# Summing all but the last key head's output products at full width in one bank, with output weights in longer runs

## The chip, the cores and the metric

The kernel runs on one core of a Trainium2 chip. The time is the device time in microseconds of one execution of the whole program, given as the median of several runs.

## What is computed

One decode step for two sequences (B = 2) of width D = 448. A layer norm of the input feeds a sliding-window attention over a key and value cache and a dense layer with a mish activation; both are added to the input. The attention has 16 query heads and 8 key heads of 256 numbers, and looks at the last 4096 positions.

```python
x = A_x                                   # (2, 1, 448), all inputs bf16
xn = _layernorm(x, axis=-1)
q = (xn @ wq)                             # 16 query heads of 256
k, v = last 4096 positions of the caches  # 8 key heads, each for two query heads
p = softmax(q @ k.T * 256 ** -0.5)
attention = (p @ v, heads side by side) @ wo       # wo: 4096 x 448
h = xn @ w1 + b1                          # 1792 wide
dense = (h * tanh(softplus(h))) @ w2
return x + attention + dense
```

The caches are by far the most of what is read: 8 key heads, each with 4 MB of K and 4 MB of V for both sequences, beside 3.5 MB of query weights, 3.1 MB of dense weights and 3.5 MB of output weights.

## The kernel before, in words

Key heads are the outer loop. For key head `i`, K and V (4 MB each) and the 448 KB of output weights that belong to its two query heads are loaded on the SP queue (`load_k`, `load_v`, `load_wo`, L349 and L366), one head ahead of their use. K and V have two buffers each, the output weights three; a load is issued when the buffer's last reader is done, and all loads queue behind each other.

A key head's 4096 positions lie as 64 rows in the 64 partitions of each sequence. They are worked on in four pieces of 16 rows (`NH` = 4 pieces, `T` = 64):

- `turn` (L373): VectorE transposes a piece of K in 32x32 blocks, one piece ahead.
- `scores` (L385): eight TensorE products of 128x512 for a piece, summed in one bank, with the query laid out block-diagonally (`qdiag`, built by GpSimd at L266). ScalarE takes the exponential in two halves (L399) and sums as it goes.
- `turn_p` (L411): VectorE transposes the exponentials of the piece before; after a head's last piece it forms the sums for the denominator (L418, L420).

After the four pieces of head `i`, the values of head `i-1` follow. `denominator` (L427) sums over partitions with an fp32 product, and VectorE takes the reciprocal (L431). Then for heads 0 to 5 `values` (L444) runs 32 products with the probabilities stationary (8 columns: two rows of positions times four (sequence, query head) pairs) and V moving, into an 8x512 bank, which ScalarE copies to `o_sb` (L452). For the last two heads (`NFIX` = 2) `values_fixed` (L494) has V stationary instead: 128 products of four columns, whose result is already transposed.

`finish` (L475 to L479) belongs to heads 0 to 5 and runs one head later, after the first piece's scores of head `i+2`: TensorE transposes the 8x512 result with four fp32 transposes, VectorE adds the two row halves, and `scale_o` (L458) multiplies by the reciprocal. `values_fixed` calls `scale_o` directly. `mix` follows: for each of two query heads and two halves of 256, the two columns of `oT` (one per sequence) are the stationary operand and the output weights move.

The sum of everything that goes to the output (the input, the dense layer, eight heads) lives in PSUM all through the kernel. `add` (L217) splits the 448 columns in four groups of 112, each on its own 32 columns of TensorE's array and its own 32 partitions of PSUM, in two banks (`psA0`, `psA1`). So each `add` is four products. At the end VectorE copies two groups to `res` and ScalarE the other two (L563), and SP stores them (L564).

`issue_in_order` ties every engine's instructions to the order in which the program writes them, so on each engine the order in the code is the order on the chip. The main loop at the end of the kernel therefore sets the order around the change: in head `i`'s iteration, loads for `i+1` and `i`, then per piece `turn` of the next, `scores`, `turn_p` of the one before, and after the first piece `close(i-2)`, which is `finish` and `mix`; after the pieces, the values of `i-1`. In the ninth iteration: `close(6)`, the values of head 7, `close(7)`.

Of the kernel before, what the change touches and what calls it, by code (L numbers as in the profile page):

```python
# [9 lines left out]
ALU = mybir.AluOpType  # L10
AXIS = mybir.AxisListType
BF16 = mybir.dt.bfloat16
FP32 = mybir.dt.float32
# [21 lines left out]
def kernel(  # L35
# [30 lines left out]
    BR = Bsz * rep  # L66
# [6 lines left out]
    ND = Dh // P  # L73
# [9 lines left out]
    ident = lead.tile([P, P], BF16)  # L83
# [15 lines left out]
    x_bf = consts.tile([Bsz, D], BF16)  # L99
# [13 lines left out]
    for lo, hi in ((0, SC), (SC, NS)):  # L113
# [4 lines left out]
    ident_f = consts.tile([Q, Q], FP32)  # L118
# [11 lines left out]
        out=rstd[:], in_=mv[:, 1:2], func=ACT.Sqrt, bias=eps_t[:], scale=1.0  # L130
# [21 lines left out]
    for j in range(1, NQ):  # L152
        nc.vector.tensor_tensor(
            out=hsel, in0=hsel, in1=ident[:, j * Q : (j + 1) * Q : HS], op=ALU.add
# [4 lines left out]
    for b in range(Bsz):  # L159
        nc.vector.tensor_reduce(  # L160
            out=off[:, b : b + 1], in_=hsel[:, b * rep : (b + 1) * rep], axis=AXIS.X, op=ALU.add
# [3 lines left out]
    nc.vector.tensor_scalar(  # L165
        out=off[:], in0=off[:], scalar1=mine[:], scalar2=1e4, op0=ALU.subtract, op1=ALU.mult
    )
    ones_f = consts.tile([P, P], FP32)
    nc.gpsimd.memset(ones_f[:], 1.0)
    NW = 2  # L170
# [8 lines left out]
    for s in range(NS):  # L179
# [7 lines left out]
        out=odd[:],  # L187
        in_=ident[:].rearrange("p (u o) -> p o u", o=2),
        axis=AXIS.X,
        op=ALU.add,  # L190
    )
    xs = consts.tile([P, NS, NX, Bsz], BF16)
    for par in range(2):
        for x in range(NX):
            which = (par + x) % 2
            nc.vector.tensor_scalar(
                out=xs[:, par : NS : 2, x, :],
                in0=xnT_ps[:, par : NS : 2, :],
# [5 lines left out]
    nc.vector.memset(ones[:], 1.0)  # L204

    NO = NQ
    DO = D // NO
    psA = [ps_a.tile([P, DO], FP32, name=f"psA{u}") for u in range(2)]  # L210

    def part(n):
        return psA[n // 2][n * Q : n * Q + Bsz, :]

    def add(lhsT, w, start=False, stop=False):
        for n in range(NO):
            nc.tensor.matmul(  # L217
                part(n),
                lhsT=lhsT,
                rhs=w[:, n * DO : (n + 1) * DO],  # L220
                start=start,
                stop=stop,
                tile_position=(0, n * Q),
                skip_group_check=True,
            )

    add(ident[0:Bsz, 0:Bsz], x_bf[:, :], start=True)


    xq = consts.tile([P, NS, NQ, Q], BF16)  # L230
# [107 lines left out]


    NSTEP = Hkv * NH  # L340
    k_t, kt_t, v_t, p_t, pT_t, wo_t = {}, {}, {}, {}, {}, {}
    state = {}

# [7 lines left out]
    def load_k(i, cuts=(0, T)):  # L351
        k_t[i] = k_pool.tile([P, T * Dh], BF16, tag="k", name="k")
        load_cache(k_t[i], A_k_cache, i, cuts)

    def load_v(i, cuts=(0, T)):
        t = v_tile()
        load_cache(t, A_v_cache, i, cuts)
        v_t[i] = t[:].rearrange("p (t d) -> p t d", t=T)

    def load_wo(kvh, parts=1):  # L360
        w = wo_pool.tile([P, rep, ND * D], BF16, tag="wo", name="wo")
        r0 = kvh * rep * Dh
        win = A_wo[r0 : r0 + rep * Dh, :].rearrange("(h p c) d -> p h (c d)", h=rep, p=P)
        for u in range(parts):
            hs = slice(u * rep // parts, (u + 1) * rep // parts)
            nc.sync.dma_start(out=w[:, hs, :], in_=win[:, hs, :])  # L366
        wo_t[kvh] = w

    def turn(s):
        kt = kt_pool.tile([P, TH * Dh], BF16, tag="kt", name="kt")  # L370
        i, half = divmod(s, NH)
        k = k_t[i] if half < NH - 1 else k_t.pop(i)
        nc.vector.transpose(  # L373
            out=kt[:].bitcast(FP32),
            in_=k[:, half * TH * Dh : (half + 1) * TH * Dh].bitcast(FP32),
        )
        kt_t[s] = kt
# [47 lines left out]
    def denominator(i):  # L425
        den = ps_m.tile([P, BR], FP32, tag="m", name="den")
        nc.tensor.matmul(  # L427
            den[:], lhsT=ones_f[:], rhs=state.pop(("sums", i))[:], start=True, stop=True
        )
        rec = small.tile([P, BR], FP32, tag="rec", name="rec")  # L430
        nc.vector.reciprocal(out=rec[:], in_=den[:])  # L431
        return rec

    NP = 2
    NR = NP * BR

    def values(i):

        po = ps_o.tile([NR, NP * Dh], FP32, tag="o", name="o")
        v = v_t.pop(i)  # L440
        state["rec", i] = denominator(i)
        for u in range(T // NP):
            piece, uh = divmod(u, TH // NP)
            nc.tensor.matmul(  # L444
                po[:],
                lhsT=pT_t[i * NH + piece][:, uh * NP * Q : (uh + 1) * NP * Q : HS],
                rhs=v[:, u * NP : (u + 1) * NP, :].rearrange("p t d -> p (t d)"),
                start=(u == 0),
                stop=(u == T // NP - 1),
            )  # L450
        o_sb = small.tile([NR, NP * Dh], FP32, tag="o_sb", name="o_sb", bufs=1)
        nc.scalar.copy(out=o_sb[:], in_=po[:])  # L452
        state["o", i] = o_sb

    def scale_o(i, o):
        rec = state.pop(("rec", i))
        oT = small.tile([P, ND, rep, Bsz], BF16, tag="oT", name="oT")
        nc.vector.tensor_tensor(  # L458
            out=oT[:].rearrange("p c h b -> p c b h"),
            in0=o.rearrange("p c (b h) -> p c b h", b=Bsz),  # L460
            in1=rec[:]
            .rearrange("p (b h) -> p b h", b=Bsz)
            .unsqueeze(1)
            .to_broadcast([P, ND, Bsz, rep]),
            op=ALU.mult,
        )
        state["oT", i] = oT

    def finish(i):
        ov = state.pop(("o", i))[:].rearrange("r (u m c) -> r u c m", u=NP, c=ND)  # L470
        pq = ps_q.tile([P, NP * ND * NR], FP32, tag="q", name="q")
        pqv = pq[:].rearrange("p (u c r) -> p u c r", u=NP, c=ND)
        for u in range(NP):
            for c in range(ND):
                nc.tensor.transpose(pqv[:, u, c, :], ov[:, u, c, :], ident_f[0:NR, 0:NR])  # L475
        o = small.tile([P, ND, BR], FP32, tag="osum", name="osum")
        nc.vector.tensor_copy(out=o[:], in_=pqv[:, 0, :, 0:BR])
        for u in range(1, NP):
            nc.vector.tensor_tensor(  # L479
                out=o[:], in0=o[:], in1=pqv[:, u, :, u * BR : (u + 1) * BR], op=ALU.add  # L480
            )
        scale_o(i, o)

    def values_fixed(i):

# [18 lines left out]
    def mix(kvh):  # L504
        oT = state.pop(("oT", kvh))
        w = wo_t.pop(kvh)
        for h in range(rep):
            for c in range(ND):
                add(
                    oT[:, c, h, :],  # L510
                    w[:, h, c * D : (c + 1) * D],
                    stop=(kvh == Hkv - 1 and h == rep - 1 and c == ND - 1),
                )

    NFIX = 2

    def close(i):
        if i < Hkv - NFIX:
            finish(i)
        mix(i)  # L520
# [7 lines left out]
    for i in range(Hkv + 1):  # L528
        if i + 1 < Hkv:
            load_k(i + 1, (0, T) if i + 1 < Hkv - 1 else (0, T // 2, T))  # L530
        if i < Hkv:
            load_v(i, (0, T) if i < Hkv - 1 else (0, T // 2, 7 * T // 8, T))
            load_wo(i, parts=1 if i < Hkv - 1 else 2)
            for piece in range(NH):
                s = i * NH + piece
                if s + 1 < NSTEP:
                    turn(s + 1)
                scores(s)
                if s >= 1:
                    turn_p(s - 1)  # L540
                if s == NSTEP - 1:
                    turn_p(s)
                if piece == 0 and i > 1:
                    close(i - 2)
            if i + 2 < Hkv:
                build_q(i + 2)
        else:
            close(i - 2)
        if i == 0:
            dense_in()  # L550
            dense_out()
        if i >= 1:
            if i - 1 < Hkv - NFIX:
                values(i - 1)
            else:
                values_fixed(i - 1)
        if i == Hkv:
            close(i - 1)
# [37 lines left out]
```

The softmax here doesn't subtract the row's maximum and nothing guards it: scores larger than these inputs give would overflow.

## Time and profile before

| | |
|---|---|
| median of 6 runs | 190.26 us (189.83 to 190.99) |
| the profiled execution's own time | 190.19 us |
| its span on the core | 188.3 us |
| mean granted TensorE clock | 0.918 |
| TensorE, VectorE, ScalarE, GpSimd busy | 136.6, 106.6, 42.5, 16.4 us |
| loads | 77.8 MB, 413 GB/s over the span |
| SP queue's share of the 16 DMA engines | 96.8% |

The span is the time from the first to the last instruction on the core; the own time also has what lies around it. In the profile PE is TensorE and PEld its weight loads, which overlap it; DVE is VectorE, ACT ScalarE, POOL GpSimd and SP the engine whose queue issues the loads. A line such as L385 is a line of the kernel. Rows of groups and of the timeline give the operation, what it writes and reads, how many there are, their time, and in brackets how long the engine had stood idle before and what ended that. The chain of what ended last is followed back from the last instruction: at each step to what released it, or to the instruction before it on its engine.

### The profile page before, as it was taken

Reading aid. Unit: us, or ns where it says so; the run is one execution under the profiler, and the core shown is the slowest. Engines: PE = TensorE matmul, PEld = TensorE weight load, DVE = VectorE, ACT = ScalarE, POOL = GpSimd, SP = SyncE. Lnnn points to the kernel's source line nnn. Section 1 sums busy time; section 2 is a strip of 40 time slices with the busy share of each in tenths; the row PEclk is TensorE's granted clock in tenths of the full one; section 3 lists DMA queues with packets and bytes.
Section 4 is the critical chain, followed back from the end, with each engine's and each line's share of the span. In section 5 each row is a group of like instructions: output and inputs, shape, how many; then the busy total and the mean of one; then the engine's idle time right before and its main releaser. Section 6 shows DMA issues by size and latency. Waiting matters only on the chain.

```text
span 188.3 us, 2587 instructions
## 1 busy us (share of the span) xinstructions
PE 136.6 (73%) x1030; PEld 65.5 (35%) x1030; DVE 106.6 (57%) x141; ACT 42.5 (23%) x142; POOL 16.4 (9%) x74
## 2 busy tenths in 40 slices
PE   0396088915989778956795589956894699988853
PEld 0132033803434333423341324322341334434852
DVE  6604597059931994089704991099407984867301
ACT  3003115200440324012421233022401233134101
POOL 7000600300020002000030003000110000000000
PEclk9999759955899999999999999999999969999955
DMA  6999999999999999999999999999999999999980
GB/s 220 420 475 439 387 448 424 442 432 445 432 439 435 405 417 441 425 439 390 469 440 432 432 432 418 435 425 423 447 428 432 411 424 428 449 445 400 419 362 26
DMA packets 5653, 77.83 MB, mean 413 GB/s; under 512 B 517, under 2 KB 2569, under 8 KB 2954
## 3 DMA queue, kind: packets, MB, share of 16 engines
q1 hardware_dynamic: 5636, 77.66, 96.8%
q8 instruction: 8, 0.13, 0.2%
q14 instruction: 3, 0.02, 0.0%
q10 hardware_dynamic: 6, 0.01, 0.0%
HBM read 77.67 MB, written 0.00 MB: 412 GB/s over the span
## 4 chain that ended last, share of the span: by engine, by line
DMA 67%; DVE 18%; PE 11%; SPq 1%; ACT 1%; issue 0%; ACTq 0%; DVEq 0%
DMA k<-in_A_k_cache_dram 57%; DVE kt L373 14%; DMA v<-in_A_v_cache_dram 10%; PE sc L385 6%; PE o L444 4%; DVE pT L411 3%; PE q L494 1%; ACT p L399 1%; PE psA L217 1%; SPq L114 0%; DVE sums L420 0%; DVE oT L458 0%; SPq L349 0%; DVE osum L479 0%; ACTq L591 0%
## 5 line engine op out<-in xcount | busy, mean ns | idle before, releaser
L373 DVE STREAM_TRANSPOSE kt<-k 128x2048 f32<-128x2048 f32 x32 | 73.1, 2288 | 53.7 <-DMA k<-in_A_k_cache_dram 53.7
L385 PE MATMUL sc<-kt,qdiag 128*128 128x512 bf16 x256 | 64.5, 399 | 22.8 <-DVE kt L373 21.7
L399 ACT ACTIVATE p<-sc,off 128x256 bf16<-128x256 f32 x64 | 33.0, 545 | 73.0 <-PE sc L385 72.3
L385 PEld LDWEIGHTS <-qdiag 128*128 128x128 bf16 x256 | 23.9, 100 | 60.8 <-issue 19.3
L444 PE MATMUL o<-v,pT 128*8 128x512 bf16 x192 | 42.5, 379 | 0.0
L444 PEld LDWEIGHTS <-pT 128*8 128x8 bf16 x192 | 17.2, 92 | 22.4
L266 POOL COPY qdiag<-qt 32x16 bf16<-32x16 bf16 x64 | 13.0, 248 | 120.3 <-PE sc L385 103.2
L411 DVE STREAM_TRANSPOSE pT<-p 128x512 bf16<-128x512 bf16 x32 | 21.5, 673 | 2.8 <-ACT p L399 2.8
L399 ACT ACTIVATION_READ_ACCUMULATOR p<-sc,off 128x1 f32 x64 | 11.8, 184 | 0.0
L452 ACT COPY o_sb<-o 8x512 f32<-8x512 f32 x6 | 3.5, 575 | 36.3 <-PE o L444 36.3
L246 PE MATMUL q_ps<-v,xq 128*128 128x512 bf16 x28 | 9.1, 502 | 2.0 <-DVE xq L237 2.0
L217 PE MATMUL psA<-wo,oT 128*2 128x112 bf16 x128 | 3.1, 220 | 9.5 <-DVE oT L458 9.5
L494 PE MATMUL q<-pT,v 128*128 128x4 bf16 x256 | 7.3, 168 | 2.6 <-DMA v<-in_A_v_cache_dram 2.6
L494 PEld LDWEIGHTS <-v 128*128 128x128 bf16 x256 | 7.1, 100 | 2.8 <-DMA v<-in_A_v_cache_dram 2.8
L256 DVE CAST q_sb<-q_ps 128x512 bf16<-128x512 f32 x2 | 1.3, 686 | 8.5 <-PE q_ps L246 8.5
L217 PE MATMUL psA<-v,act_bf 128*2 128x112 bf16 x56 | 1.5, 296 | 6.3 <-DVE act_bf L331 6.3
L246 PEld LDWEIGHTS <-xq 128*128 128x128 bf16 x28 | 3.4, 123 | 7.3 <-issue 3.8
L217 PEld LDWEIGHTS <-oT 128*2 128x2 bf16 x128 | 1.6, 81 | 10.2 <-DVE oT L458 10.2
L180 PE MATMUL xnT_ps<-ident,xn_bf 2*128 2x2 bf16 x7 | 0.5, 166 | 5.7 <-DVE xn_bf L138 5.7
L458 DVE TENSOR_TENSOR oT<-q,rec 128x8 bf16<-128x8 f32 x2 | 0.3, 166 | 7.4 <-PE q L494 7.4
L475 PEld LDWEIGHTS q<-ident_f,o_sb 8*128 8x128 f32 x24 | 3.3, 207 | 2.6 <-issue 2.6
L256 ACT CAST q_sb<-q_ps 128x512 bf16<-128x512 f32 x2 | 1.1, 588 | 12.4 <-PE q_ps L246 12.4
(54 smaller groups left out, 46.9 us busy)
## 6 DMA issues: line engine op xcount, KB each, us to landing
k<-in_A_k_cache_dram SPq DMA_DIRECT2D x7, 4096.0 KB, 29.6
v<-in_A_v_cache_dram SPq DMA_DIRECT2D x7, 4096.0 KB, 29.9
k<-in_A_k_cache_dram SPq DMA_DIRECT2D x2, 2048.0 KB, 24.5
v<-in_B_w_dram SPq DMA_DIRECT2D x2, 1568.0 KB, 24.6
wo<-in_A_wo_dram SPq DMA_DIRECT2D x7, 448.0 KB, 30.4
v<-in_A_wq_dram SPq DMA_DIRECT2D x1, 2048.0 KB, 7.6
v<-in_A_v_cache_dram SPq DMA_DIRECT2D x1, 2048.0 KB, 14.9
v<-in_A_wq_dram SPq DMA_DIRECT2D x1, 1536.0 KB, 10.7
```

The source lines that it names most:

```text
L217: nc.tensor.matmul(part(n), lhsT=lhsT, rhs=w[:, n * DO : (n + 1) * DO], start=start, stop=stop, tile_position=(0, n * Q), skip_group_check ...
L246: nc.tensor.matmul(ps[u][:], lhsT=xq[:, s, :, :].rearrange("p j k -> p (j k)"), rhs=wq_sb[:, s, u * N5 : (u + 1) * N5], start=(s == 0), st ...
L256: copy(out=q_sb[:, u * N5 : (u + 1) * N5], in_=ps[u][:])
L266: nc.gpsimd.tensor_copy(out=tv[rows, :, e, j * Q : (j + 1) * Q : HS].rearrange("p n (b h) -> p n b h", b=Bsz), in_=qv[rows, :, h0 : h0 + r ...
L373: nc.vector.transpose(out=kt[:].bitcast(FP32), in_=k[:, half * TH * Dh : (half + 1) * TH * Dh].bitcast(FP32),)
L385: nc.tensor.matmul(psc[:], lhsT=qdiag[i % NW][:, n * NE + e, :], rhs=ktv[:, n, e, :, :], start=(n == 0 and e == 0), stop=(n == NB - 1 and ...
L399: nc.scalar.activation(out=pv[:, b, :, :], in_=sv[:, b, :, :], func=ACT.Exp, scale=scale, bias=off[:, b : b + 1], accum_out=state["rs", i] ...
L411: nc.vector.transpose(out=pT[:], in_=p_t.pop(s)[:])
L444: nc.tensor.matmul(po[:], lhsT=pT_t[i * NH + piece][:, uh * NP * Q : (uh + 1) * NP * Q : HS], rhs=v[:, u * NP : (u + 1) * NP, :].rearrange ...
L452: nc.scalar.copy(out=o_sb[:], in_=po[:])
L475: nc.tensor.transpose(pqv[:, u, c, :], ov[:, u, c, :], ident_f[0:NR, 0:NR])
L494: nc.tensor.matmul(po[:, c, :], lhsT=vv[:, t, c, :], rhs=pTv[:, th, 0:Q:HS], start=(t == 0 and c == 0), stop=(t == T - 1), skip_group_chec ...
```

## The change

There are four edits.

1. The sum of the output gets a full-width bank of its own, `psE` (2 partitions, 448 columns). The input, the dense layer and heads 0 to 6 are added there, by one product of 448 columns for each `add`. The last head alone uses the four column groups (`add_last`), which now lie in one bank `psA`.
2. `carry`, after head 6's output products in the ninth iteration, copies `psE` to SBUF on VectorE and starts the four column groups with it, by four fp32 products with a 2x2 identity.
3. The output weights of heads 0 to 5 are loaded so that each partition takes four consecutive rows (3584 bytes in one run) in place of two rows (1792 bytes) for each of two query heads. Query head 0 then has partitions 0 to 63, query head 1 has 64 to 127.
4. To match this, the result of heads 0 to 5 must be transposed with each query head on its half of the partitions. `values` copies the 8x512 result to `o_sb` twice as large, in two ScalarE copies with every 64 columns repeated for both query heads; `finish` makes eight fp32 products with `o_sb` stationary, which also add the two row halves, in place of the four transposes; VectorE multiplies by the reciprocal, multiplies by `own` (1 where the partition's half is the query head's, else 0) and adds the two query heads. `own` is formed once in the prologue by two VectorE reductions.

```diff
+    own = consts.tile([P, Bsz, rep], FP32)
+    for h in range(rep):
+        nc.vector.tensor_reduce(
+            out=own[:, :, h],
+            in_=ident[:, h * PH : (h + 1) * PH].unsqueeze(1).to_broadcast([P, Bsz, PH]),
...
+    psE = ps_a.tile([Bsz, D], FP32, name="psE")
+    def add(lhsT, w, start=False, stop=False):
+        nc.tensor.matmul(
+            psE[:], lhsT=lhsT, rhs=w, start=start, stop=stop, skip_group_check=True
+        )
...
-    psA = [ps_a.tile([P, DO], FP32, name=f"psA{u}") for u in range(2)]
+    psA = ps_a.tile([P, DO], FP32, name="psA")
...
+    def carry():
+        early = consts.tile([Bsz, D], FP32, name="early")
+        nc.vector.tensor_copy(out=early[:], in_=psE[:])
+        add_last(ident_f[0:Bsz, 0:Bsz], early[:, :], start=True)
...
+        if kvh < Hkv - NFIX:
+            nc.sync.dma_start(
+                out=w[:].rearrange("p h n -> p (h n)"),
+                in_=A_wo[r0 : r0 + rep * Dh, :].rearrange("(p j) d -> p (j d)", p=P),
+            )
+            return
...
-        nc.scalar.copy(out=o_sb[:], in_=po[:])
+        for u in range(NP):
+            nc.scalar.copy(
+                out=o_sb[:, u, :, :, :],
+                in_=po[:, u * Dh : (u + 1) * Dh]
+                .rearrange("r (m j) -> r j m", j=NJ)
+                .unsqueeze(2)
+                .to_broadcast([NR, NJ, rep, PH]),
+            )
...
-        for u in range(NP):
-            for c in range(ND):
-                nc.tensor.transpose(pqv[:, u, c, :], ov[:, u, c, :], ident_f[0:NR, 0:NR])
+        for j in range(NJ):
+            for u in range(NP):
+                nc.tensor.matmul(
+                    pqv[:, j, :],
+                    lhsT=o_sb[:, u, j, :, :].rearrange("r h m -> r (h m)"),
+                    rhs=ident_f[0:NR, u * BR : (u + 1) * BR],
+                    start=(u == 0 and j == 0),
+                    stop=(u == NP - 1),
...
+        put = add_last if kvh == Hkv - 1 else add
+        if kvh < Hkv - NFIX:
+            for j in range(NJ):
+                add(oT[:, j, :], w[:].rearrange("p h (c d) -> p (h c) d", c=ND)[:, j, :])
+            return
...
             close(i - 2)
+            carry()
```

More of the change, by code (lines that the diff above doesn't have):

```diff
@@ L167 @@
     )
+    PH = P // rep
+    own = consts.tile([P, Bsz, rep], FP32)
[3 more added lines that the diff above has]
+            in_=ident[:, h * PH : (h + 1) * PH].unsqueeze(1).to_broadcast([P, Bsz, PH]),
+            axis=AXIS.X,
+            op=ALU.add,
+        )
     ones_f = consts.tile([P, P], FP32)
@@ L204, with add_last @@
     nc.vector.memset(ones[:], 1.0)
+    psE = ps_a.tile([Bsz, D], FP32, name="psE")
[3 more added lines that the diff above has]
+        )
+    add(ident[0:Bsz, 0:Bsz], x_bf[:, :], start=True)
     NO = NQ
     DO = D // NO
-    psA = [ps_a.tile([P, DO], FP32, name=f"psA{u}") for u in range(2)]
+    psA = ps_a.tile([P, DO], FP32, name="psA")
     def part(n):
-        return psA[n // 2][n * Q : n * Q + Bsz, :]
-    def add(lhsT, w, start=False, stop=False):
+        return psA[n * Q : n * Q + Bsz, :]
+    def add_last(lhsT, w, start=False, stop=False):
         for n in range(NO):
@@ L225, in add @@
             )
-    add(ident[0:Bsz, 0:Bsz], x_bf[:, :], start=True)
+    def carry():
+        early = consts.tile([Bsz, D], FP32, name="early")
+        nc.vector.tensor_copy(out=early[:], in_=psE[:])
+        add_last(ident_f[0:Bsz, 0:Bsz], early[:, :], start=True)
     xq = consts.tile([P, NS, NQ, Q], BF16)
@@ L340 @@
     NSTEP = Hkv * NH
+    NFIX = 2
     k_t, kt_t, v_t, p_t, pT_t, wo_t = {}, {}, {}, {}, {}, {}
@@ L362, in load_wo @@
         r0 = kvh * rep * Dh
+        wo_t[kvh] = w
+        if kvh < Hkv - NFIX:
[4 more added lines that the diff above has]
+            return
         win = A_wo[r0 : r0 + rep * Dh, :].rearrange("(h p c) d -> p h (c d)", h=rep, p=P)
@@ L366, in load_wo @@
             nc.sync.dma_start(out=w[:, hs, :], in_=win[:, hs, :])
-        wo_t[kvh] = w
     def turn(s):
@@ L432, in denominator @@
         return rec
+    NJ = Dh // PH
+    assert rep == 2 and NJ == rep * ND
     NP = 2
@@ L450, in values @@
             )
-        o_sb = small.tile([NR, NP * Dh], FP32, tag="o_sb", name="o_sb", bufs=1)
-        nc.scalar.copy(out=o_sb[:], in_=po[:])
+        o_sb = small.tile([NR, NP, NJ, rep, PH], FP32, tag="o_sb", name="o_sb", bufs=1)
+        for u in range(NP):
[5 more added lines that the diff above has]
+                .to_broadcast([NR, NJ, rep, PH]),
+            )
         state["o", i] = o_sb
@@ L469, in finish @@
     def finish(i):
-        ov = state.pop(("o", i))[:].rearrange("r (u m c) -> r u c m", u=NP, c=ND)
-        pq = ps_q.tile([P, NP * ND * NR], FP32, tag="q", name="q")
-        pqv = pq[:].rearrange("p (u c r) -> p u c r", u=NP, c=ND)
-        for u in range(NP):
-            for c in range(ND):
[L475 to L482, printed above, removed]
+        o_sb = state.pop(("o", i))
+        pq = ps_q.tile([P, NJ * BR], FP32, tag="q", name="q")
+        pqv = pq[:].rearrange("p (j r) -> p j r", j=NJ)
+        for j in range(NJ):
[6 more added lines that the diff above has]
+                    stop=(u == NP - 1),
+                    skip_group_check=True,
+                )
+        rec = state.pop(("rec", i))
+        o = small.tile([P, NJ, Bsz, rep], FP32, tag="osum", name="osum")
+        nc.vector.tensor_tensor(
+            out=o[:].rearrange("p j b h -> p j (b h)"),
+            in0=pqv,
+            in1=rec[:].unsqueeze(1).to_broadcast([P, NJ, BR]),
+            op=ALU.mult,
+        )
+        nc.vector.tensor_tensor(
+            out=o[:].rearrange("p j b h -> p j (b h)"),
+            in0=o[:].rearrange("p j b h -> p j (b h)"),
+            in1=own[:].rearrange("p b h -> p (b h)").unsqueeze(1).to_broadcast([P, NJ, BR]),
+            op=ALU.mult,
+        )
+        oT = small.tile([P, NJ, Bsz], BF16, tag="oTm", name="oTm")
+        nc.vector.tensor_tensor(
+            out=oT[:], in0=o[:, :, :, 0], in1=o[:, :, :, 1], op=ALU.add
+        )
+        state["oT", i] = oT
     def values_fixed(i):
@@ L506, in mix @@
         w = wo_t.pop(kvh)
+        put = add_last if kvh == Hkv - 1 else add
[3 more added lines that the diff above has]
+            return
         for h in range(rep):
             for c in range(ND):
-                add(
+                put(
                     oT[:, c, h, :],
                     w[:, h, c * D : (c + 1) * D],
-                    stop=(kvh == Hkv - 1 and h == rep - 1 and c == ND - 1),
+                    stop=(kvh >= Hkv - 2 and h == rep - 1 and c == ND - 1),
                 )
-    NFIX = 2
     def close(i):
```

## The prediction

> **What bounds the kernel now.** I read the slices first, then the chain of what ended last, then the last 40 us as a timeline, then the groups for prices.
>
> ```profile
> span 188.3 us, 2587 instructions
> PE 136.6 (73%) x1030; PEld 65.5 (35%) x1030; DVE 106.6 (57%) x141; ACT 42.5 (23%) x142; POOL 16.4 (9%) x74
> ...
> DMA  6999999999999999999999999999999999999980
> ```
>
> The DMA row is 9 from the second slice to the last but one; the page gives 77.83 MB at a mean of 413 GB/s, and the SP queue's share of the 16 engines is 96.8%. No compute engine is near that, so the kernel is a stream of loads that must not run dry, plus what is left when the last load lands. The chain's end says how much that is:
>
> ```profile
> 163.74 0.54 SPq L349
> ...
> 164.33 18.38 DMA v<-in_A_v_cache_dram
> 182.71 0.05 issue
> 182.76 1.89 PE q L494 x64
> 184.65 0.02 issue
> 184.67 0.18 DVE oT L458
> 184.84 0.04 issue
> 184.89 0.65 PE psA L217 x16
> 185.54 0.23 ACT res L563
> ```
>
> After 182.7 us a fixed tail of 5.6 us runs: 64 of the last head's value products, a scaling, the output products, the copies and the store. TensorE reached that tail with little to spare, which a 73% average hides. The timeline of the stretch before:
>
> ```profile
> 163.75 0.57 ACT L452 COPY o_sb<-o 8x512 f32<-8x512 f32 x1 [6.05 <-PE o L444]
> ...
> 165.48 0.64 PE L475 MATMUL q<-ident_f,o_sb 8*128 8x8 f32 x4
> ...
> 166.16 0.17 DVE L477 COPY osum<-q 128x8 f32<-128x8 f32 x1 [1.99 <-PE q L475]
> ...
> 171.87 1.89 PE L385 MATMUL sc<-kt,qdiag 128*128 128x512 bf16 x8 [0.89 <-DVE kt L373]
> ...
> 177.52 0.37 PE L217 MATMUL psA<-wo,oT 128*2 128x112 bf16 x16 [0.26 <-DVE oT L458]
> ...
> 178.65 1.87 PE L494 MATMUL q<-pT,v 128*128 128x4 bf16 x64 [0.37 <-DMA v<-in_A_v_cache_dram]
> ...
> 182.76 1.87 PE L494 MATMUL q<-pT,v 128*128 128x4 bf16 x64 [2.23 <-DMA v<-in_A_v_cache_dram]
> ```
>
> The last two brackets are the whole reserve: TensorE waited 0.37 us for the first half of the last V and 2.23 us for the rest, 2.6 us in all. Anything added on TensorE, or on VectorE ahead of it, after the last K has landed (158 us) eats from that. Earlier heads are different: each K lands, TensorE sits 2.3 to 2.4 us until it is transposed (idle before L385 at 103.9, 124.4 and 145.1 us), and the V and K issues run 8 to 18 us ahead of the queue.
>
> [...] The packet records of this trace agree: 1792 bytes take 74 ns, 4096 bytes 159, 32768 bytes 1213. [...] loads of 128 bf16 columns take 100 ns (L385), of fp32 192 (L427) and 207 (L475). [...] The trace shows two records for each (L427: x16 for eight heads), while an fp32 transpose is one (L475: x24 for six heads of four). [...] At 149.22 us the 16 column-group products start within 0.16 us, and the next score product 0.30 us after the first[...].
>
> **The change, part by part.**
>
> *Output weights in 3584-byte runs, heads 0 to 5.* 256 packets of 1792 bytes become 128 of 3584, for six heads, so each of 16 engines handles 6x8 = 48 packets fewer. A line through the durations above has a fixed part of about 8 ns; start to start on one engine at the end of the stream I read 70.5 ns, for a fixed part of 4.5 ns. Saving: 48x4.5 = 0.22 to 48x8 = 0.38 us; I take 0.3 at the end of the stream, 0.2 at K of head 6. The stream is the bound, so all of it counts if nothing else becomes last. The SP issues stay as many, at the same places.
>
> *Full-width summing.* Sixteen products of 112 columns held TensorE 0.30 us a head (149.22 to 149.52); eight score products of 512 columns take 1.90 us of which the last is 0.40, so one streams in 1.5/7 = 0.215 us, one of 448 columns in 0.19, and four in 0.75. So +0.45 us a head. For heads 0 to 5 it is covered by the waits for transposed K behind it (0.57 and 0.89 us a head). The dense layer's 56 products become 14: 1.48 us before, 2.7 at full clock, 5.2 at half (the granted clock is 0.59 there); TensorE is up to 3.7 us later at 46 us, which the 2.4 us of wait per head uses up within three heads, while V's issue there is 11 us ahead of the queue.
>
> *The new finish.* Four fp32 transposes become eight fp32 products, two passes each: 16. The transposes start 0.12 us apart; the only two back-to-back fp32 passes (L427 at 177.82 us) start 0.108 apart. I take 0.12: 15x0.12+0.28 = 2.08 us, against 0.64: +1.44 on TensorE. Bounds: 0.105 a pass (+1.2) and 0.217 (+2.9), the latter if weight load and product don't overlap, as at L427 at 156.2 us. VectorE's three small operations become three others of the same size (0.16 to 0.17 us each): nothing. ScalarE's one copy of 0.57 us becomes two, 1.15: it ends at 164.9 where the finish starts at 165.5, so it is covered by the score products; if they read slower by over 0.3 us each, the finish waits.
> Behind VectorE's first of the three stands the next K transpose, so a late finish moves all that follows. In a head with late K, VectorE reaches it only at 148.6 us and the old transposes were done by 147.6: of +1.44, 0.43 is left. In the last head VectorE already waits 1.99 us for TensorE: the full 1.44 counts.
>
> *The carry.* After head 6's output products (in TensorE's order ahead of the last denominator and all of the last head's value products), VectorE copies 2x448 and TensorE waits. The copy: 112 columns took 0.26 us (L563), 512 took 0.69 (L256), so 0.62 for 448. With the end latency of the product before it (0.16) and two hand-overs (0.04 and 0.05), 0.87 us; then four fp32 products in column groups: 0.1 us if the groups overlap[...]; I take 0.3. Sum 1.17 (0.95 to 1.6).
>
> *Two reductions for `own` in the prologue*: 0.28 us each as L186; the projection starts 0.5 us later, but the first scores wait for K until 24.03 with the query ready at 21.2. Nothing.
>
> *The last head* still uses column groups, in one bank. Its copies read different partitions. Nothing.
>
> **Sum.** From K of head 6 on: -0.2 (stream) +0.43 (finish, head 4) +1.44 (finish, head 5) +0.45 (output products, head 6) +1.17 (carry) = +3.3 us on TensorE. Head 5's output products hide in the 0.89 us wait at 171.87. The reserve is 2.6, so the second half of the last values starts 0.7 late. Against that, at the end: the output products began at 184.89 and stalled 0.1 for the last weights (the second load landed at 185.02), a wait that goes; [...]the last 16 take 0.37 as in other heads rather than 0.54: -0.27. Net +0.4 us, on a span of 188.3 and an own time of 190.19; the 1.9 around the span stays. The median shown is 190.26, so 190.65.
>
> **Rivals.**
> *A, TensorE takes the end over from the stream by a little (forecast, 0.48):* 190.65, itself 190.0 to 191.2.
> *B, the stream stays the bound (0.20).* Speaks for it: passes at 0.105 us take 0.45 off the sum (0.2 in each of two heads and a little more), and a carry of 0.95 takes 0.2. Then what is gained is the packets and the wait for the last weights: 190.26-0.3-0.1 = 189.85; with the largest saving and a full clock, 189.6.
> *C, slower (0.32): the fp32 finish.* Place: line 475's successor in heads 4 and 5. Every 0.01 us on a pass adds 0.15 us in each of the two heads, so the time passes 0.3% (190.83) from 0.13 us a pass on. At 0.217 the sum is -0.2+1.9+2.9+0.45+1.17 = 6.2, less 2.6 and 0.27: +3.3, 193.6. Midway, 0.16, gives 191.8. For it: no run of weight loads of this form is in the trace[...]. Against: the transposes load the same 128 fp32 columns every 0.12 us.
>
> **How the numbers follow.** A measurement of this kernel tells about 0.3% from no change. A and B mostly fall inside it (A's upper part above, B's lower part below): faster 0.10, same 0.48, slower 0.42. The range runs from 189.7 (B) to 192.4 (C beyond midway).
>
> **What would show it.** In the profile after: 16 finish passes spanning about 2.1 us; VectorE's wait for them in the last head grown from 2.0 to about 3.4; the copy to `early` at about 0.6 with TensorE idle 0.9 around it; the wait of 2.23 us for V gone, and the chain's end running through TensorE back to head 5's finish; 3584-byte packets near 140 ns. If the wait for the rest of V still stands, B is right. If the finish spans over 2.5 us, C is. I am wrong altogether if the DMA row shows a gap before the end, or the copies on ScalarE delay the finish.

## The result and the profile after

The median of 15 runs is 191.82 us (190.99 to 193.44), against 190.21 us for 34 runs of the kernel before. The ratio is 1.0099, with a 95% interval of 1.0079 to 1.0119: slower by about 1%, 1.6 us. The forecast of 190.65 us had the direction and lay within 0.3% of no change; the measured loss is larger than that and inside the range of 189.7 to 192.4.

Not all of this lies in the span on the core. The spans have a median of 190.0 us (189.1 to 190.9), against 188.4 in 112 runs of the kernel before; what lies around the span is 1.8 to 3.3 us here (10 of 15 runs over 1.9) and 1.7 to 1.9 before. By the means, 1.5 us of the loss is in the span and 0.5 around it, where the profile shows nothing; the cause of that part stays open.

The profiled execution took 192.56 us with a span of 190.7, so it lies in the upper half of the runs and shows more of the loss than a typical run. From the page of the kernel after, the clock, the loads and the chain:

```profile
span 190.7 us, 2498 instructions
PE 157.3 (82%) x981; PEld 75.8 (40%) x981; DVE 109.1 (57%) x144; ACT 45.3 (24%) x148; POOL 16.3 (9%) x74
...
PEclk9999558855799997999999879996999699978855
DMA  6999999998999999999999999999999999999940
...
PE 48%; DMA 34%; DVE 12%; SPq 1%; ACT 1%; issue 1%; ACTq 0%; DVEq 0%
```

TensorE has 49 records fewer and is 20.7 us busier. The stream of loads has no gap (the DMA row) and its last packet ends 0.55 us earlier than before, as far as the packet records show (184.11 against 184.66 us). But the chain is now 48% TensorE, where it was 11%. Before:

```profile
DMA 67%; DVE 18%; PE 11%; SPq 1%; ACT 1%; issue 0%; ACTq 0%; DVEq 0%
```

The end of the chain in the kernel after, in order of time:

```profile
169.42 7.00 PE sc L416 x24
176.42 0.12 PE den L458 x2
176.54 3.42 PE q L554 x128
...
180.21 1.67 PE psE L220 x4
181.88 0.02 issue
181.90 0.62 DVE early L249
182.52 0.04 issue
182.56 0.55 PE psA L237 x8
183.11 0.52 PE den L458 x2
183.63 3.43 PE q L554 x128
187.06 0.02 issue
187.09 0.18 DVE oT L498
187.26 0.04 issue
187.31 0.65 PE psA L237 x10
```

There is no load in it: the last head's 128 value products run in one piece, and the wait of 2.23 us for the rest of V is gone. What TensorE did in the two heads before, from its timeline (start, duration, line, shapes, count, idle before):

```profile
146.47 1.94 PE L516 MATMUL q<-ident_f,o_sb 8*128 8x4 f32 x16
...
149.09 1.65 PE L220 MATMUL psE<-wo,oTm 128*2 128x448 bf16 x4 [0.68 <-DVE oTm L539]
...
165.88 1.94 PE L516 MATMUL q<-ident_f,o_sb 8*128 8x4 f32 x16
...
167.86 0.18 DVE L526 TENSOR_TENSOR osum<-q,rec 128x16 f32<-128x16 f32 x1 [3.92 <-PE q L516]
...
168.50 0.92 PE L220 MATMUL psE<-wo,oTm 128*2 128x448 bf16 x4 [0.68 <-DVE oTm L539]
...
169.35 7.07 PE L416 MATMUL sc<-kt,qdiag 128*128 128x512 bf16 x24
...
180.21 1.65 PE L220 MATMUL psE<-wo,oT 128*2 128x448 bf16 x4 [0.26 <-DVE oT L498]
```

The sixteen fp32 passes take 1.94 us. The four full-width products take 0.92 us once and 1.65 us twice, for the same work: the clock. The windows before and behind the two finishes, and that of head 6's products and the carry, with the granted clock in the column before the last two:

```profile
core 0: us, PE busy (x) PEld busy (x) DVE busy (x) ACT busy (x) POOL busy (x), PEclk, DMA share, GB/s
145.00:149.10 4.10, 3.42 (x25) 2.34 (x23) 3.79 (x10) 1.07 (x4) 0.00 (x0) 1.00 1.09 472
149.10:152.50 3.40, 3.40 (x9) 1.03 (x10) 3.40 (x3) 0.00 (x0) 0.00 (x0) 0.50 0.86 360
164.00:169.60 5.60, 4.92 (x31) 2.92 (x31) 1.67 (x4) 2.12 (x6) 0.00 (x0) 1.00 1.06 456
169.60:173.00 3.40, 3.40 (x10) 1.15 (x9) 3.40 (x3) 0.23 (x1) 0.00 (x0) 0.50 0.85 350
179.90:183.00 3.10, 2.14 (x14) 0.44 (x12) 0.78 (x2) 0.00 (x0) 0.00 (x0) 0.50 0.89 355
```

After each of these two finishes TensorE gets half its clock for 3.4 us, most of it in score products. In the records of the clock such an interval of 3.41 us follows the finish in five of six heads (70.6, 108.2, 128.7, 149.1, 169.6 us). In the kernel before there is one in the steady part (150.7 us). The half clock of the last window is another one: it begins at 179.9 us and lasts to the end, and it follows no finish but the 128 value products of head 6 (176.40 to 179.95). In the kernel before it begins at 178.0 us, when head 6's output products (177.52 to 177.82) are done.

### The profile page after: what moved, and what is told of

It reads as the page before. It is cut to its first block, busy times and chain, and to the rows that moved or that the text cites. A ratio compares the mean times of both kernels' runs of the same rounds, so it can differ in the third digit from the quotient of the medians.

```text
span 190.7 us, 2498 instructions
## 1 busy us (share of the span) xinstructions
PE 157.3 (82%) x981; PEld 75.8 (40%) x981; DVE 109.1 (57%) x144; ACT 45.3 (24%) x148; POOL 16.3 (9%) x74
## 4 chain that ended last, share of the span: by engine, by line
PE 48%; DMA 34%; DVE 12%; SPq 1%; ACT 1%; issue 1%; ACTq 0%; DVEq 0%
DMA k<-in_A_k_cache_dram 34%; PE sc L416 18%; PE o L477 15%; DVE kt L404 8%; PE psE L220 6%; PE q L516 5%; PE q L554 4%; DVE pT L442 1%; PE psA L237 1%; PE den L458 1%; ACT p L430 1%; DVE osum L526 0%; DVE osum L532 0%; DVE oTm L539 0%; SPq L114 0%
## 5 line engine op out<-in xcount | busy, mean ns | idle before, releaser
L416 PE MATMUL sc<-kt,qdiag 128*128 128x512 bf16 x256 | 67.1, 419 | 11.0 <-DVE kt L404 10.3
L416 PEld LDWEIGHTS <-qdiag 128*128 128x128 bf16 x256 | 25.4, 104 | 53.3 <-issue 24.5
L477 PEld LDWEIGHTS <-pT 128*8 128x8 bf16 x192 | 17.2, 92 | 22.4
L486 ACT COPY o_sb<-o 8x512 f32<-8x512 f32 x12 | 6.3, 572 | 36.3 <-PE o L477 36.3
L516 PEld LDWEIGHTS q<-ident_f,o_sb 8*128 8x128 f32 x96 | 11.1, 186 | 2.5 <-issue 2.5
L516 PE MATMUL q<-ident_f,o_sb 8*128 8x4 f32 x96 | 11.7, 249 | 0.0
L220 PE MATMUL psE<-wo,oTm 128*2 128x448 bf16 x24 | 7.7, 460 | 4.1 <-DVE oTm L539 4.1
L220 PE MATMUL psE<-v,act_bf 128*2 128x448 bf16 x14 | 5.4, 574 | 6.5 <-DVE act_bf L354 6.5
L269 PE MATMUL q_ps<-v,xq 128*128 128x512 bf16 x28 | 8.1, 461 | 2.1 <-DVE xq L260 2.1
L526 DVE TENSOR_TENSOR osum<-q,rec 128x16 f32<-128x16 f32 x6 | 1.0, 175 | 8.6 <-PE q L516 8.6
L220 PEld LDWEIGHTS <-act_bf 128*2 128x2 bf16 x14 | 1.6, 120 | 9.6 <-DVE act_bf L354 6.6
```

The source lines that it names most:

```text
L220: nc.tensor.matmul(psE[:], lhsT=lhsT, rhs=w, start=start, stop=stop, skip_group_check=True)
L269: nc.tensor.matmul(ps[u][:], lhsT=xq[:, s, :, :].rearrange("p j k -> p (j k)"), rhs=wq_sb[:, s, u * N5 : (u + 1) * N5], start=(s == 0), st ...
L416: nc.tensor.matmul(psc[:], lhsT=qdiag[i % NW][:, n * NE + e, :], rhs=ktv[:, n, e, :, :], start=(n == 0 and e == 0), stop=(n == NB - 1 and ...
L477: nc.tensor.matmul(po[:], lhsT=pT_t[i * NH + piece][:, uh * NP * Q : (uh + 1) * NP * Q : HS], rhs=v[:, u * NP : (u + 1) * NP, :].rearrange ...
L486: nc.scalar.copy(out=o_sb[:, u, :, :, :], in_=po[:, u * Dh : (u + 1) * Dh] .rearrange("r (m j) -> r j m", j=NJ) .unsqueeze(2) .to_broadcas ...
L516: nc.tensor.matmul(pqv[:, j, :], lhsT=o_sb[:, u, j, :, :].rearrange("r h m -> r (h m)"), rhs=ident_f[0:NR, u * BR : (u + 1) * BR], start=( ...
```

## The experiments

**Theory T**: TensorE's chain from the last K on has outgrown its reserve of 2.6 us, by the finish, the full-width products and the carry together. Rivals: **F**, the fp32 finish alone is the loss; **G**, the carry and the full-width products alone; **S**, the full-width dense layer puts TensorE late for good; **H**, a large part of the loss is the half clock after each finish. Each kernel was timed beside the kernel before.

### The old finish with the full-width sum

```diff
-        if kvh < Hkv - NFIX:        # wo in 3584-byte runs, new finish
+        if False:
...
+                nc.tensor.transpose(pqv[:, u, c, :], ov[:, u, c, :], ident_f[0:NR, 0:NR])
```

> The changed kernel with heads 0 to 5 finished as before (four fp32 transposes, output weights in 1792-byte runs, one copy of the result); the full-width sum and the carry stay. Theory T (TensorE's chain from the last K on, which has to fit in a reserve of 2.6 us): takes off about 1.3 us in head 5, gives the packets back (0.2 to 0.3 us), and adds only the full-width products and the carry (2.5 us or less) to the reserve: 190.0 to 190.6. Rival G (the carry and full-width products alone are the loss): stays at 191.3 to 191.9. Rival S (the full-width dense layer makes the start late for good): stays at 191.5 to 191.9.

Measured: 190.00 us, ratio 0.9996 (0.9987 to 1.0006). G falls: the full-width sum and the carry alone cost nothing.

### The new finish with the column groups

```diff
-    psE = ps_a.tile([Bsz, D], FP32, name="psE")
+    add = add_last
...
-            carry()
```

> The changed kernel with everything summed in the four column groups as before (in one bank), no full-width sum and no carry; the new finish and the 3584-byte runs stay. Theory T: takes the carry (1.2 us) and head 6's full-width products (0.45 us at full clock, 1.3 at half) off; the finish alone (+1.3 in head 5, up to 0.5 in head 4) fits in the reserve: 189.8 to 190.4. Rival F (the fp32 finish alone is the loss): 191.2 to 191.8. Rival S: 189.9 to 190.3, like T.

Measured: 190.06 us, ratio 1.0000 (0.9989 to 1.0012). F falls as well. Either half of the change fits in the reserve, taking off 1.8 us; only both together come out late. It fits with nothing left over: in both profiles TensorE runs the last head's 128 value products without a wait for V and ends them at 184.9 us (the old finish) and 184.6 (the groups), where the kernel before ended them at 184.63.

### The dense layer in the column groups

```diff
-                add(act_bf[:, c, x, :], w2_sb[:, x, c, :])
+                add_last(act_bf[:, c, x, :], w2_sb[:, x, c, :])
```

> The changed kernel with the input and the dense layer summed in the four column groups as before; heads 0 to 6 stay at full width and the carry is added to the groups. Theory T: the dense layer's lateness (5.4 us of TensorE in place of 1.5, at 45 us) is used up long before the last K: 191.5 to 192.1, no change. Rival S (the start stays late): 190.0 to 190.5.

Measured: 192.72 us, ratio 1.0130 (1.0114 to 1.0146). S falls: giving the start its 3.9 us back gains nothing. That it is slower than the changed kernel no theory expected; its profile has a stall of 0.91 us with nothing to wait for, 17 products before the end of head 6's values (179.62 us). Less the stall it would be 191.8, an estimate, still near the changed kernel and far from the 190.5 of S. Stalls of this kind come up again below.

### The finish in bf16

```diff
-        o_sb = small.tile([NR, NP, NJ, rep, PH], FP32, tag="o_sb", name="o_sb", bufs=1)
+        o_sb = small.tile([NR, NP, NJ, rep, PH], BF16, tag="o_sb", name="o_sb", bufs=1)
...
-                    rhs=ident_f[0:NR, u * BR : (u + 1) * BR],
+                    rhs=ident[0:NR, u * BR : (u + 1) * BR],
```

> The changed kernel with the result of heads 0 to 5 copied as bf16 and the eight products of the finish in bf16: one pass in place of two[...]. It rounds the unscaled attention result to bf16 once more than the reference. Theory T: the finish takes about 0.5 us in place of 1.9: -1.4 us in head 5 and some 0.2 to 0.5 in head 4: 190.0 to 190.6. Rival G: 191.3 or more. Rival H (the loss is the half clock that follows each finish, set off by its long stretch of little work): the stretch shrinks to what it was before, so the clock should rise from 0.88 to about 0.91 and the time fall to 190.2 as well; then the profile tells by which of the two.

Measured: 189.89 us, ratio 0.9982 (0.9972 to 0.9991): faster than before by a little. The profiled run took 189.51 us, and TensorE's timeline in it reads:

```profile
164.78 0.35 PE L516 MATMUL q<-ident,o_sb 8*128 8x4 bf16 x8
165.80 0.92 PE L220 MATMUL psE<-wo,oTm 128*2 128x448 bf16 x4 [0.68 <-DVE oTm L539]
...
178.21 0.55 PE L237 MATMUL psA<-early,ident_f 2*2 2x112 f32 x8 [0.70 <-DVE early L249]
...
182.10 1.87 PE L554 MATMUL q<-pT,v 128*128 128x4 bf16 x64 [1.12 <-DMA v<-in_A_v_cache_dram]
```

The finish is down to 0.35 us, the wait for the rest of V is back with 1.12 us to spare, and no half clock lies between 48 and 178 us (mean 0.929). The stream of loads sets the end again, 0.3 us earlier than before. The run cannot separate passes from clock, since both went.

### A warm TensorE after each finish

```diff
+        junk = ps_o.tile([P, 512], FP32, tag="o", name="junk")
+        for again in range(3):
+            nc.tensor.matmul(junk[:], lhsT=ident[:, :], rhs=..., start=True, stop=True)
```

> The changed kernel with three products of 128x512 into an unused bank, 0.65 us, after each finish's passes, where TensorE waits 0.68 us for VectorE; their result is not used. Rival H (the half clock after each finish is a large part): the clock stays full after the finish, the full-width products take 0.9 in place of 1.65 us and the scores behind them are faster: 190.3 to 191.2, clock 0.90 or more. Theory T with the passes and waits alone: no gain, 191.8 to 192.3.

Measured: 190.72 us in nine runs, ratio 1.0035 (1.0021 to 1.0049); a tenth run took 193.38. This separates them: the passes are all there and TensorE has more to do, and yet 1.1 of the 1.6 us is gone. In the span alone the median falls from 190.0 to 188.9. In the profile (of a run of 190.72 us):

```profile
165.60 1.94 PE L516 MATMUL q<-ident_f,o_sb 8*128 8x4 f32 x16
167.70 0.59 PE L526 MATMUL junk<-xq,ident 128*128 128x512 bf16 x2 [0.16 <-issue]
168.23 0.92 PE L220 MATMUL psE<-wo,oTm 128*2 128x448 bf16 x4
169.08 3.66 PE L416 MATMUL sc<-kt,qdiag 128*128 128x512 bf16 x16
...
179.00 0.92 PE L220 MATMUL psE<-wo,oT 128*2 128x448 bf16 x4 [0.26 <-DVE oT L498]
```

(The trace has two records for the three added products.) The clock is full from 115 us to the carry, after one half-clock stretch of 10.2 us, the full-width products take 0.92 us in every late head, and the score products run at full speed behind the finish. The added products also shift the instructions behind them, but the changed kernel's profile has no stall behind the last K that this could have moved away. H holds: about two thirds of the loss went with the half clock.

### The finish done twice in head 5, and in heads 0 to 3

```diff
+        for again in range(2 if i == 5 else 1):      # the other kernel: i < 4
+            for j in range(NJ):
```

> The changed kernel with the sixteen fp32 passes of head 5's finish done twice (the second overwrites the first with the same numbers). Theory T: TensorE's chain sets the end, so the full 1.87 us is added: 193.5 to 193.9. If the stream of loads or another engine sets it, 191.8 to 192.3.

> The changed kernel with the fp32 passes of the finish done twice in heads 0 to 3 (7.5 us of TensorE in all), not in heads 4 and 5. Theory T: what these heads lose is waited off at the next K; the last reset is K of head 6, where 1.0 us of waiting is left in the profile after, so 0 to 1 us is seen: 191.8 to 192.8. A kernel bound by TensorE throughout would show all: 199.

Measured: 194.75 us for head 5 (median of four runs, 192.56 to 194.97; two more, at a clock of 0.858 in place of 0.891 or above, took 195.51 and 196.15), 1.024 times the kernel before; 199.42 us, ratio 1.0480 (1.0461 to 1.0499), for heads 0 to 3. The first shows that TensorE sets the end, but adds 2.9 us, not the 1.87 of the passes. Fastest run against fastest run it adds 1.6 (192.56 and 190.99). Its only profile is of that fastest run, so where the rest lies stays open. The second is a miss for T: all of the 7.5 us arrives, when all but 1 should have been waited off at a K. Its chain:

```profile
PE 69%; DMA 19%; DVE 8%; SPq 1%; issue 1%; ACT 1%; ACTq 0%; DVEq 0%
```

The issues of V, which wait for the end of a head's values, show the greater part of the reason: through the four doubled heads they come 22.4, 21.2, 21.0 and 22.4 us apart (64.9 to 152.0 us), while K lands every 20.46. In the kernel after, the same four are 19.4, 18.5, 20.0 and 20.4 apart (65.4 to 143.7): TensorE is still catching up there and has little to wait off. From 60 us to the last K it stands waiting ahead of a score product four times, for 0.59, 0.70, 0.95 and 0.99 us, 3.2 in all, where the kernel before stood 2.1 to 2.4 us for each K from 83 to 145 us. With the doubled finish the wait is gone in all four places. So 4.3 of the 7.5 us have to arrive. For the other 3.2 there is a candidate that no run separates: from 60 to 149 us the clock is half for 20.5 us, against 10.2 in the changed kernel.

### The carry's copy placed early

```diff
-        put = add_last if kvh == Hkv - 1 else add
+        put = add_last if kvh >= Hkv - NFIX else add
...
+            if i == Hkv - 1:
+                save()                                # early <- psE, after head 7's pieces
```

> The changed kernel with the full-width sum ended after head 5: the copy to SBUF is placed on VectorE after head 7's pieces, where nobody waits for it, heads 6 and 7 go to the column groups, and the fp32 products stay where they were. Theory T: takes 0.9 us of waiting and the difference of head 6's full-width products (0.45 to 1.3 us) off TensorE's chain: 190.0 to 190.6. Rivals F and S: 191.2 or more.

Measured: 191.72 us (190.78 to 192.00), ratio 1.0076 (1.0057 to 1.0096): no gain that can be told from the changed kernel, against the expectation. The span on the core does gain: its median is 189.1 us, against 190.0. The time around it hides that, with 2.6 to 2.8 us in three of the six runs. The waits are gone as meant, but TensorE's timeline (of the fastest run, 190.78 us) has a new one:

```profile
179.83 0.37 PE L237 MATMUL psA<-early,ident_f 2*2 2x112 f32 x8
180.13 0.39 PE L461 MATMUL den<-sums,ones_f 128*128 128x4 f32 x2
180.37 0.19 PE L557 MATMUL q<-pT,v 128*128 128x4 bf16 x2
181.79 3.50 PE L557 MATMUL q<-pT,v 128*128 128x4 bf16 x126 [1.22 <-issue]
```

Two products into the last head's values it stands for 1.22 us with nothing that the profile shows to wait for ("issue"). The packet records have a block of 16384 bytes on the queue "q8 instruction" starting at 179.43 us, and the next at 182.93. The kernel before has 8 such blocks and 2060 records of TensorE (1030 products, 1030 weight loads), the changed kernel 7 and 1962: 258 to 280 TensorE instructions a block, an estimate that counts the other engines' as none.

### The same, and the changed kernel, with every later TensorE instruction moved by 128 places

```diff
     project()
+    pads = ps_q.tile([Bsz, Bsz], FP32, tag="q", name="pads")
+    for again in range(64):
+        nc.tensor.matmul(pads[:], lhsT=ident[0:Bsz, 0:Bsz], rhs=ident[0:Bsz, 0:Bsz], ...)
```

> The kernel with the carry's copy placed early and heads 6 and 7 in the column groups, and besides 64 tiny products into an unused place right after the query projection, where TensorE waits 6 us for the first K anyway; they shift every later TensorE instruction by 128 places. In the profile without them TensorE stood 1.22 us with nothing to wait for, two products into the last head's values, and an instruction block of 16 KB was fetched just then. Theory I (that stall is a late fetch of instructions, and took the place of the carry's wait): it moves to another place ahead of the wait for V, and the gain that was missed appears: 190.3 to 191.0. If the stall belongs to the values or to the early copy, it stays and the time too: 191.5 to 191.9.

> The changed kernel with the same 64 tiny products after the projection and nothing else: the control. Theory I: in the changed kernel a block was fetched at 180.2 us, behind the wait for the carry, so moving it gives at most a stall where there was none or nothing: 191.4 to 192.8. If the tiny products themselves[...] gain anything, it is seen here as under 191.3.

Measured: 190.94 us (190.19 to 192.01), ratio 1.0046 (1.0025 to 1.0068), for the early carry, and 192.48 us (191.12 to 193.18), ratio 1.0119 (1.0089 to 1.0149), for the control. TensorE's timeline of the first:

```profile
180.33 2.02 PE L557 MATMUL q<-pT,v 128*128 128x4 bf16 x66
183.38 1.79 PE L557 MATMUL q<-pT,v 128*128 128x4 bf16 x62 [1.03 <-issue]
```

The stall comes after 66 products in place of 2: 64 products, or 128 instructions with their loads, further. With 256 instructions a block, near the estimate above and the distance of two stalls in the last experiment (128 products with their loads), the program grew by half a block and the stall moved by half a block. So it belongs to the blocks in which instructions are fetched, as far as that estimate holds. What it waits for inside a fetch is not shown: the block's packet was through at 180.36 us, and the stall without the tiny products runs from 180.56 to 181.79. Where it moved to was not as expected (ahead of the wait for V); it stayed inside the last values. So the move gained nothing in the span (median 189.0 us, against 189.1), and most of the difference in time lies around the span; the two intervals overlap. The control shows no gain from the tiny products.

### The bf16 finish with the early carry, without and with the 64 tiny products

```diff
-        o_sb = small.tile([NR, NP, NJ, rep, PH], FP32, tag="o_sb", name="o_sb", bufs=1)
+        o_sb = small.tile([NR, NP, NJ, rep, PH], BF16, tag="o_sb", name="o_sb", bufs=1)
...
-        put = add_last if kvh == Hkv - 1 else add
+        put = add_last if kvh >= Hkv - NFIX else add
```

The rest of both edits, and the tiny products of the second, are as shown above.

> The bf16 finish and the early carry together, without the tiny products; the result of heads 0 to 5 is rounded once more to bf16. With the bf16 finish alone TensorE still waited 1.12 us for the rest of the last V, so the stream of loads set its end. Theory: nothing is left to gain on TensorE, 189.7 to 190.0, as with the bf16 finish alone (189.89). If a fetch of instructions falls on the last values it can be 190.1 to 190.5.

> The same with the 64 tiny products, so that the instruction blocks end elsewhere: 189.7 to 190.0 if the stream of loads sets the end; the two differ by more than 0.2 us only if a fetch stall reaches the end in one of them.

Measured: 189.74 us, ratio 0.9984 (0.9974 to 0.9995), and with the tiny products 190.69 us, ratio 1.0025 (1.0015 to 1.0035). The first ends where the bf16 finish alone did: the stream is the bound, and the carry's place has no price there. The second is slower by 0.95 us, by instructions that run at 20 us beside a wait of 6. In its profile (of its fastest run) TensorE's last values:

```profile
178.19 0.26 PE L237 MATMUL psA<-wo,oT 128*2 128x112 bf16 x4 [1.33 <-issue]
...
179.31 1.90 PE L557 MATMUL q<-pT,v 128*128 128x4 bf16 x64
182.05 1.54 PE L557 MATMUL q<-pT,v 128*128 128x4 bf16 x50 [0.84 <-DMA v<-in_A_v_cache_dram]
184.11 0.53 PE L557 MATMUL q<-pT,v 128*128 128x4 bf16 x14 [0.53 <-issue]
```

A stall of 0.53 us lies 14 products from the end, behind the last wait for V, where nothing covers it. Without the tiny products the same stall is 0.21 us and lies exactly 64 products earlier, ahead of that wait. The stall of 1.33 us lies 128 products, a whole block by that estimate, before the other; the wait for V behind it covers it. The two profiled runs are 0.6 us apart.

## Why the prediction was right, and where its sizes were off

The profiled runs, span 188.3 before and 190.7 after; times in us. The run after lies 0.74 us above its median, so the sizes are those of a run with more loss than the typical 1.6.

| term of the sum | forecast | measured |
|---|---|---|
| stream, at K of head 6 | -0.2 | -0.45 (142.64 to 142.19) |
| head 4: finish, seen at VectorE | +0.43 | +0.29 |
| head 4: products and the scores behind them | 0 | +0.53 (149.22 to 165.48; 149.09 to 165.88) |
| head 5: finish | +1.44 | +1.30 (0.64 to 1.94) |
| head 5: products and the scores behind them | 0 | +0.93 (166.77 to 173.61; 168.50 to 176.26) |
| head 6: full-width products | +0.45 | +1.37 (0.30 to 1.67) |
| carry | +1.17 | +1.16 (181.88 to 183.04) |
| reserve | 2.6 | used up |
| tail | -0.27 | about 0 |
| end of the last values | +0.7 | +2.42 (184.63 to 187.05) |

*What held.* The likeliest rival A: TensorE takes the end over from the stream. The finish's sixteen passes, which start 0.113 us apart against 0.12 forecast, and the carry to a hundredth. The packets: 3584 bytes take 140 ns, and bursts of output weights come 20.46 us apart in place of 20.50, 0.04 a head, at the lower end of the estimate. Rival B's time, 189.85 us if the stream stays the bound, is what the bf16 finish gives (189.89). The dense layer's lateness is used up before the end, though in five heads and not three (V's issue is 3.7 us later than before at 84.8, 1.0 at 143.7).

*What failed.* The term "+0.45 us a head" for the full-width products, and what was to hide them: "the 0.89 us wait" in head 5 and the 0.57 us in head 4. All were sized at full clock. The measured terms add up to 5.1 us on TensorE, 1.8 more than the 3.3 forecast: 0.92 more for head 6's products, 0.93 for head 5's products and the scores behind them, 0.53 for those of head 4, less 0.5 for the stream and the two finishes. Half clock is in all three: 3.4 us behind each finish, and all of head 6's products, in the half clock that begins at 179.9 us. The kernel before has that stretch too, from 178.0; now the products are wider and later and fall into it. In the tail the forecast went the other way, with 0.37 us in place of 0.54 for the last sixteen products, by an estimate of the author's. The last values now run without a pause (183.49 to 187.05), and the clock is half all the same: 0.50 from 179.85 us to the end, and the last sixteen take 0.54. In the finish TensorE has more to do, but of a thin kind: 16 passes on 8 rows and the wait behind them stretch the part of each head with little work from about 2.6 us (146.92 to 149.52 before) to 3.4 (146.47 to 149.9, had the products run at full clock). In the records of both kernels every half-clock interval but the last, which runs to the end, is 3.41 us or a multiple. That a thin stretch sets the half clock off fits the added products: with them the clock is 1.00 from 149.2 to 156.6 us and from 167.7 to 175.1, where the changed kernel has 0.78 (149.1 to 157.0 and 168.5 to 176.2). How long or how thin it has to be is not shown: the 3.41 us ahead of 149.13 still hold 0.82 us of score products. That the added products, with the passes still there, bring back 1.1 us is shown.

Where the half clock falls is what counts. The old finish with the full-width sum has three such intervals in its profile and the new finish with the groups five, the last at 150.4 us in both, and both are free: none lies behind the last finish, where no wait for K makes up for it.

*Rival C* (passes dearer than 0.13 us) was wrong in its cause, though its sign came true. That 191.82 lies inside the range is luck in part: the upper end was set for dear passes, which did not come, and the half clock that filled the room had no place in the sum.

*The reserve* was right to be the hinge: each half of the change alone is free within 0.1%, and both are 1% slower. But a reserve at the end is not the only one; each late head had 2.4 us and was left 1.0 (the wait for K at 145.1 us before and at 144.7 after), and the earlier ones less, which the doubled finish in heads 0 to 3 makes plain.

## What to carry to other kernels

An engine that waits a little in every stage can take new work for nothing up to the sum of its waits, and at full price or more from there on; read the reserve where the stream ends, and per stage. Price added products at the clock that the stretch around them will get: small fp32 passes are busy time that did not keep TensorE's clock up (0.50 for 3.41 us behind five of six finishes), and a shorter form of the same step (bf16, one pass, 0.35 us in place of 1.94) turned a loss of 1% into a gain of 0.2%. When a stall reads "issue" with nothing behind it, look at the instruction queue before explaining it by the edit (here a block of 16384 bytes started 1.1 us ahead of a stall of 1.22).

## What the runs showed of the hardware that was not expected

- Half-clock intervals of 3.41 us come back 20.48 us apart (108.17, 128.65, 149.13, 169.61 us), six times their length, and the bursts of output weights 20.46 apart, so the intervals nearly keep their place in the head (they begin 2.4 to 3.7 us after the start of a finish). Whether that place differs from run to run, which would explain why the changed kernel's span spreads over 1.8 us (189.1 to 190.9), is a guess of the author's, not shown. It fits that the control's profile, of a run of 191.12 us, has full clock from 153.7 to 181.1 us and takes 0.92 us for head 6's products. It cannot explain the rest of the spread, which lies around the span.
- Fetches of instructions (16384 bytes each, 0.88 to 0.96 us a packet but for one of 1.36 in the profiles before and after) go with stalls of TensorE of 0.2 to 1.3 us in the last 12 us, where it goes through 256 instructions in as little as 3.5 us. The stalls begin 1.0 to 2.1 us after the packet does, and many fetches have none. Where they fall depends on how many instructions stand before: 64 tiny products in the prologue moved the time by 0.95 us.
- Placing work off the path can uncover such a stall: in the changed kernel a fetch started at 180.24 us, when TensorE was about to wait for the carry; with that wait gone, the stall of 1.22 us stood in its place. That the wait covered it is argued: the kernel with the groups, which has no carry to wait for either, has a stall of 1.05 us in the last values (180.57 to 181.62), and no profile with the wait has one there.
